# Another layout for loading and transposing queries and keys in a fused attention, soft-MoE and feed-forward kernel

## The chip, the cores and the metric

The kernel runs on one core of a Trainium2 chip. The metric is the device time of one execution in microseconds (us). A core has five engines with queues of their own: PE (TensorE, matrix products and transposes, results into PSUM), DVE (VectorE), ACT (ScalarE), POOL (GpSimd) and SP (SyncE, which here only issues transfers). Sixteen DMA engines move data between HBM and the on-chip memory, SBUF. Both on-chip memories have 128 partitions; an operand is so many partitions by so many elements. PEld is PE's loading of the stationary operand.

## The reference, cut to what matters

Three parts follow each other: an attention over q, k and v of shape (4 batches, 8 heads, 576 tokens, 64), a soft mixture of experts over its output, and a feed-forward layer. Only the first reads q and k:

```
q_d, k_d, v_d = means over 4 neighbouring tokens
out_d     = softmax(q_d k_d^T / 8) v_d              # 144 x 144 per head
scores    = q k^T / 8 where |i - j| < 4, else -1e9  # a band of 7
out_local = softmax(scores) v
out = repeat(out_d, 4 tokens) + out_local
x = out as (4 * 576 tokens, 8 heads * 64)
x = soft_moe(x; phi, w1, w2)          # 8 experts, 4 slots each
y = relu(x w_in)^2 w_out
```

The products need q and k with the 64 channels of a head on the partitions and tokens along the free dimension, while HBM holds a token's channels side by side. So q and k are transposed on the chip.

## The kernel before

The attention works on sixteen units; a unit is two heads of one batch. A loop takes a step for each unit, and a step works on several units at once: it transposes unit s, computes scores of unit s-1 and the values of units s-2 and s-3. The order of the work inside a step is written out by hand as a string of letters, `ORDER = "VDTAQL4gSpsEvdmqwenGtNlc"`; each engine gets its instructions in that order and runs them in order. The letters that matter here:

- `Q` (`load_qk`, lines 333 to 342): SP issues the loads of q and k of unit s+2, one each. A load brings 576 tokens of both heads to 96 partitions, three blocks of two neighbouring tokens per head on each, so that a contiguous run is two tokens, 512 bytes. There are two buffers for q and two for k, so the load waits until the transposes of unit s have read theirs.
- `L` and `4` (`load_v`, `load_v4`): SP issues the windows of v that the local attention reads (two loads in runs of 256 bytes) and the v block that is averaged over four tokens (runs of 2 KB) for unit s-1. `l` issues two or three weight loads for the experts and the feed-forward part, 512 KB each. SP's queue is served in order, so all of these stand in one line.
- `T` (`transposes`, lines 375 to 387): for q and k and each head, three transposes of 96 partitions into one PSUM bank, then two copies to SBUF, one for the even and one for the odd tokens, each 64 partitions by 288 elements, written with a step of two elements. ACT makes six of the eight copies, DVE the two of the second head's k. The PSUM buffers of the tag "t" are three banks, which the transposes share with the letters `p`, `q` and `t` (probabilities and outputs).
- `d` (line 389): POOL sums four neighbouring tokens of the transposed q and k. It stands behind `v` in POOL's queue (line 480, first sum of the v block, which waits for the load of `4`); `w` (line 486, DVE) is its second sum, and `D` (line 521, PE) multiplies with it.
- `S` (line 409): the local scores on PE; on DVE their maxima (417) and differences (418), on ACT their exponential `E` (423). `A` (line 534, DVE) adds the two attentions' values; it stands behind the copies of `T` on DVE. `g` and `G` (lines 602 to 630), every fourth step, gather the slot inputs of a finished batch. `c` converts pieces of the feed-forward weights on DVE, a number per step that a table gives.

Queries and keys are written into `qs[u % 2]`, both heads on 128 partitions, and `kzs[u % 2]`, where each head has columns of its own, with zeros on the other head's partitions. Columns 3 to 578 hold the 576 tokens in order. A table of units before the loop (`START`) does the first three units (T0, T1, T2), `DRAIN` the work after the last. Then follow the experts and the feed-forward part, which take the rest of the time.

Of the kernel before, what the change touches and what calls it, by code (L numbers as in the profile page):

```python
# [9 lines left out]
F32 = mybir.dt.float32  # L10
# [8 lines left out]
B, H, S, D = 4, 8, 576, 64  # L19
# [50 lines left out]
def attention_moe_ffn_kernel(  # L70
# [12 lines left out]
    nc = tc.nc  # L83
    cp = ctx.enter_context(tc.tile_pool(name="const", bufs=1))
    ring = ctx.enter_context(tc.tile_pool(name="ring", bufs=1))
# [5 lines left out]
    def bank(tag, shape, bufs, name, dt=F32):  # L91
        return ps.tile(shape, dt, tag=tag, bufs=bufs, name=name)

    def bt(shape, name):
        return bank("t", shape, 3, name)
# [4 lines left out]
    ident = cp.tile([128, 128], F32, name="ident")  # L100
# [5 lines left out]
    for g in range(4):  # L106
        r = slice(32 * g, 32 * g + 32)
# [186 lines left out]
    with tc.tile_pool(name="att", bufs=1, side="right") as ap:  # L294
        NV = 2
        vws, qs, kzs = [], [], []
        for i in range(NV):

            t = ap.tile([128, NB, D], F32, name=f"vw{i}")
# [3 lines left out]
        for i in range(2):  # L303
            t = aq.tile([128, SP + 6], F32, name=f"q{i}")
# [4 lines left out]
            t = aq.tile([128, 2, SP + 6], F32, name=f"kz{i}")  # L309
# [23 lines left out]
        def load_qk(u):  # L333
            b, hp = divmod(u, NP)
            h0 = 2 * hp
            st = U[u]
            for nm, src in (("q", q), ("k", k)):

                t = ring.tile([128, 1024], F32, tag=f"{nm}{u % 2}", name=f"{nm}{u}")[0:96, 0:768]
                t = t.rearrange("p (h a c) -> p h a c", h=2, a=3)  # L340
                nc.sync.dma_start(out=t, in_=src[b, h0:h0 + 2].rearrange("h (a p r) d -> p h a (r d)", a=3, r=2))
                st[nm] = t

        def load_v(u):
# [29 lines left out]

        def transposes(u):
            st = U[u]
            for j, nm in enumerate("qk"):
                for h in range(2):

                    t = bt([128, 3, 96], f"tr{u}_{j}{h}")  # L380
                    for i in range(3):
                        nc.tensor.transpose(t[:, i], st[nm][:, h, i], ident[0:96, 0:96])  # L382
                    hr = slice(64 * h, 64 * h + 64)
                    to = (kzs[u % 2][hr, h] if j else qs[u % 2][hr])[:, 3:3 + S].rearrange("p (i c r) -> p i c r", i=3, r=2)
                    for r in range(2):
                        copy = nc.vector.tensor_copy if j and h else nc.scalar.copy
                        copy(out=to[:, :, :, r], in_=t[64 * r:64 * r + 64])  # L387

        def downsample(u):
            eng = nc.vector if u in DDVE else nc.gpsimd  # L390
# [258 lines left out]
        def gate_rows(b):  # L649
# [6 lines left out]
            else:  # L656
# [8 lines left out]
                nc.vector.tensor_tensor(out=ctt_lo, in0=m, in1=ctt_hi, op=ALU.subtract)  # L665

        load_qk(0)
        for x in LOADS.split():
            if x[0] == "l":
                load_next(int(x[1:]))  # L670
            elif x == "phi":
                nc.sync.dma_start(out=phis, in_=phi.rearrange("(c p) s -> p c s", p=128))
            else:
                dict(Q=load_qk, L=load_v)[x[0]](int(x[1:])) if x[0] != "4" else load_v4(int(x[1:]))
# [3 lines left out]
        tm.enter_context(tc.manual_schedule())  # L678
        step = {
            "V": values, "T": transposes, "D": values_down, "A": value_adds, "Q": load_qk,  # L680
            "L": load_v, "S": scores_local, "p": probs_local, "E": exp_local, "s": scores_down, "d": downsample,
            "v": value_sums, "m": max_down, "q": probs_down, "e": exp_down, "n": norm_local, "N": norm_down,
# [52 lines left out]
        t = bt([1, 128], "mtp")  # L735
# [4 lines left out]
        t = bt([128, 2], "mbp")  # L740
# [23 lines left out]
        t = bt([128, 4, 32], "stp")  # L764
# [47 lines left out]
    for i in range(2):  # L812
        t = xp.tile([128, 2, 4, NS], F32, name=f"ht{i}")
# [221 lines left out]
    for i in range(2, len(steps) + LOOK):  # L1035
        up = lambda name, shape: pf.tile(shape, F32, tag="up", bufs=2, name=name)
        for x in SLOTS.get(i, ()):
            j = int(x[1:])
# [6 lines left out]
        if i < len(steps):  # L1045
            c, f = steps[i]
# [38 lines left out]
```

## Time and profile before

| | |
|---|---|
| Time, median of 3 runs | 465.41 us (463.23 to 468.02) |
| The profiled execution | 468.44 us, of which its span (first to last instruction) 466.7 us |
| PE busy | 423.5 us (91%) |
| DVE busy | 307.8 us (66%) |
| ACT busy | 262.0 us (56%) |
| POOL busy | 113.9 us (24%) |
| Mean granted clock of PE | 0.96 |
| DMA | 75.20 MB in 63,852 packets: 24,250 under 512 bytes, 42,938 under 2 KB |

The profile is of one execution on the chip. An instruction has a line of the kernel, an engine and the tiles that it writes and reads (`tr<-ident,k`: writes tr, reads ident and k). Idle time of an engine before an instruction is put down to what released it. Busy shares are averages over the whole span, in which the attention is less than half; so the views that follow are of stretches of it. The granted clock is the share of full speed that PE's throttle gave.

### The profile page before, as it was taken

The page shows a single profiled execution, that of the slowest core. Times are in us where ns is not written, and L with a number is a line of the kernel's source. Part 1 is how long each engine was busy: PE and PEld are TensorE (multiplying, and loading weights), DVE is VectorE, ACT ScalarE, POOL GpSimd, SP SyncE. Part 2 cuts the span into 40 slices and gives each one's busy share as a digit, 9 for nine tenths or more (in the row PEclk, how much of TensorE's full clock was granted, in tenths as well). Part 3 has the DMA queues.
Part 4 walks back from the last instruction along what each step waited for, and adds up shares of the span by engine and source line. Part 5 has one row for each costly group of instructions (what it writes and reads, how often), then busy time and mean ns, then how long its engine had stood idle before and what let it go on. Part 6 is the DMA issues. An engine that isn't in the chain of part 4 may idle for free.

```text
span 466.7 us, 10636 instructions
## 1 busy us (share of the span) xinstructions
PE 423.5 (91%) x4098; PEld 324.4 (70%) x4098; DVE 307.8 (66%) x655; ACT 262.0 (56%) x665; POOL 113.9 (24%) x173
## 2 busy tenths in 40 slices
PE   6489879886997988999869999999999999999996
PEld 5377666675675665454547787788888888888885
DVE  5488778796999993142398999946545555446542
ACT  5358765555676642124569897885445445444442
POOL 5158666655867840011000000000000000000000
PEclk9789979898999899899998999999999999999999
DMA  9999999999999978999996000003001001001001
GB/s 181 198 314 212 219 236 215 198 240 242 277 232 232 266 236 269 400 399 388 409 409 256 0 2 0 2 0 136 0 0 70 0 2 67 0 1 68 2 1 67
DMA packets 63852, 75.20 MB, mean 161 GB/s; under 512 B 24250, under 2 KB 42938, under 8 KB 63802
## 3 DMA queue, kind: packets, MB, share of 16 engines
q1 hardware_dynamic: 63658, 74.39, 58.4%
q8 instruction: 32, 0.52, 0.5%
q14 instruction: 18, 0.15, 0.1%
q10 hardware_dynamic: 144, 0.13, 0.1%
HBM read 69.79 MB, written 4.72 MB: 160 GB/s over the span
## 4 chain that ended last, share of the span: by engine, by line
PE 55%; DVE 20%; DMA 15%; issue 3%; ACT 3%; POOL 2%; SPq 1%; DVEq 0%; POOLq 0%; ACTq 0%
PE po L1014 37%; DMA v<-in_v_dram 13%; PE hp L822 4%; PE so L846 3%; PE up L954 3%; DVE win L217 2%; POOL v L480 2%; DVE win L218 2%; DVE vd L486 2%; DMA k<-in_k_dram 1%; DVE sm L450 1%; DVE glo L967 1%; DVE w L217 1%; DVE xt L534 1%; DVE win L215 1%
## 5 line engine op out<-in xcount | busy, mean ns | idle before, releaser
L1014 PE MATMUL po<-wparts,ghi 128*128 128x512 f32 x576 | 150.5, 395 | 4.3 <-DVE wparts L912 4.1
L1014 PEld LDWEIGHTS po<-wparts,ghi 128*128 128x128 f32 x576 | 107.2, 189 | 26.7 <-DVE wparts L912 6.6
L959 ACT ACTIVATE r<-up 128x384 f32<-128x384 f32 x96 | 47.0, 490 | 71.9 <-PE up L954 67.0
L1014 PE MATMUL po<-wparts,glo 128*128 128x512 f32 x288 | 82.2, 393 | 0.5 <-DVE glo L967 0.5
L963 DVE TENSOR_TENSOR r<-r 128x384 f32<-128x384 f32 x64 | 35.6, 557 | 58.6 <-ACT ghi L962 58.6
L967 DVE TENSOR_TENSOR glo<-r,ghi 128x384 fp32r<-128x384 f32 x94 | 52.3, 557 | 16.5 <-ACT ghi L966 10.3
L1014 PEld LDWEIGHTS po<-wparts,glo 128*128 128x128 f32 x288 | 54.3, 189 | 12.5 <-DVE glo L967 1.1
L962 ACT ACTIVATE ghi<-r 128x384 fp32r<-128x384 f32 x66 | 34.7, 526 | 2.1
L954 PE MATMUL up<-cst,ast 128*128 128x384 f32 x96 | 33.1, 346 | 0.4 <-DVE ast L945 0.4
L387 ACT COPY q<-tr 64x288 f32<-64x288 f32 x64 | 26.7, 418 | 10.9 <-PE tr L382 10.1
L480 POOL TENSOR_TENSOR v<-v 72x512 f32<-72x512 f32 x16 | 21.3, 1333 | 31.7 <-DMA v<-in_v_dram 31.7
L459 POOL TENSOR_TENSOR pl<-el,sm 64x350 f32<-64x350 f32 x30 | 26.0, 867 | 10.2 <-PE xrp L564 4.8
L387 DVE COPY kz<-tr 64x288 f32<-64x288 f32 x32 | 14.6, 457 | 14.9 <-PE tr L382 14.5
L382 PE MATMUL tr<-ident,k 96*128 96x96 f32 x96 | 16.4, 294 | 8.6 <-ACT q L387 8.3
L382 PE MATMUL tr<-ident,q 96*128 96x96 f32 x96 | 13.4, 285 | 9.7 <-DMA q<-in_q_dram 5.4
L508 PE MATMUL av<-pt,vw 64*64 64x58 f32 x640 | 22.0, 219 | 0.1
L508 PEld LDWEIGHTS av<-pt,vw 64*64 64x64 f32 x640 | 19.9, 135 | 2.9 <-issue 1.8
L954 PEld LDWEIGHTS up<-cst,ast 128*128 128x128 f32 x96 | 18.1, 189 | 4.6 <-DVE ast L945 0.7
L395 POOL TENSOR_TENSOR s<-kz 64x288 f32<-64x288 f32 x30 | 20.4, 678 | 2.3
L475 ACT COPY pt<-ptp 128x512 f32<-128x512 f32 (+1 forms) x32 | 12.1, 429 | 15.5 <-PE ptp L474 15.5
L382 PEld LDWEIGHTS tr<-ident,k 96*128 96x128 f32 x96 | 11.3, 165 | 12.0 <-ACT q L387 11.3
L467 POOL TENSOR_TENSOR pd<-pd,sm 128x432 f32<-128x432 f32 x16 | 16.4, 1028 | 10.9 <-DVE sm L451 9.9
(188 smaller groups left out, 714.2 us busy)
## 6 DMA issues: line engine op xcount, KB each, us to landing
w<-in_moe_w_dram SPq DMA_DIRECT2D x64, 512.0 KB, 8.1
win<-in_moe_w_in_dram SPq DMA_DIRECT2D x16, 512.0 KB, 9.0
wout<-in_moe_w_out_dram SPq DMA_DIRECT2D x16, 512.0 KB, 10.5
vw<-in_v_dram SPq DMA_DIRECT2D x30, 160.0 KB, 6.0
q<-in_q_dram SPq DMA_DIRECT2D x16, 288.0 KB, 10.3
k<-in_k_dram SPq DMA_DIRECT2D x16, 288.0 KB, 5.7
out_dram<-o SPq DMA_DIRECT2D x17, 256.0 KB, 2.2
v<-in_v_dram SPq DMA_DIRECT2D x16, 256.0 KB
```

Source lines behind the costliest of these rows:

```text
L382: nc.tensor.transpose(t[:, i], st[nm][:, h, i], ident[0:96, 0:96])
L387: copy(out=to[:, :, :, r], in_=t[64 * r:64 * r + 64])
L395: eng.tensor_tensor(out=s1[r], in0=t[:, :, 0], in1=t[:, :, 1], op=ALU.add)
L459: (nc.vector if u in NDVE else nc.gpsimd).tensor_tensor(out=pl[r, :, c0:c0 + W], in0=el[r], in1=sm[r, 0:NB].unsqueeze(2).to_broadcast([64, ...
L480: nc.gpsimd.tensor_tensor(out=v4[:, :, 0], in0=v4[:, :, 0], in1=v4[:, :, 1], op=ALU.add)
L508: nc.tensor.matmul(av[a][rr, 2 * HQ * i:2 * HQ * i + 2 * HQ].rearrange("p (f c) -> p f c", f=2), vw[rr, 2 * i + a], ptv[rr, i, :, a, 0:HQ] ...
L954: nc.tensor.matmul(t, ast[:, 128 * f:128 * f + 128], cst[:, c * n:c * n + n], start=True, stop=True)
L959: nc.scalar.activation(out=r, in_=t, func=AF.Relu)
L962: nc.scalar.activation(out=ghi, in_=r, func=AF.Square)
L963: nc.vector.tensor_tensor(out=g, in0=r, in1=r, op=ALU.mult)
L967: nc.vector.tensor_tensor(out=glo, in0=g, in1=ghi, op=ALU.subtract)
L1014: nc.tensor.matmul(po[c][i], a[:, 128 * i:128 * i + 128], w[f], start=(f == 0 and w is whi and a is ghi), stop=(f == NF - 1 and a is glo), ...
```

## The change

q and k of a unit are loaded to all 128 partitions: partition p of a head (64 partitions for each of the two heads) gets tokens 9p to 9p+8, one contiguous run of 2,304 bytes. A transpose then takes one token of the nine for both heads: 128 partitions by 64 channels become 64 partitions by 128 columns, of which 64 belong to each head. Four such transposes fill one PSUM bank, interleaved, so that four neighbouring tokens stand side by side; each writes every fourth word. Copies take 64 partitions by 256 elements for one head, in runs of four tokens with a step of nine. The ninth token has a tile for itself, for q and k together, written without gaps; DVE copies it in four pieces of 64 elements. A unit has eighteen transposes where it had twelve, five PSUM tiles where it had four, and twelve copies where it had eight.

```diff
             for nm, src in (("q", q), ("k", k)):
 
-                t = ring.tile([128, 1024], F32, tag=f"{nm}{u % 2}", name=f"{nm}{u}")[0:96, 0:768]
-                t = t.rearrange("p (h a c) -> p h a c", h=2, a=3)
-                nc.sync.dma_start(out=t, in_=src[b, h0:h0 + 2].rearrange("h (a p r) d -> p h a (r d)", a=3, r=2))
+                t = ring.tile([128, 1024], F32, tag=f"{nm}{u % 2}", name=f"{nm}{u}")[:, 0:9 * D]
+                nc.sync.dma_start(out=t, in_=src[b, h0:h0 + 2].rearrange("h (p t) d -> (h p) (t d)", t=9))
                 st[nm] = t
...
         def transposes(u):
             st = U[u]
+            to = []
+            for h in range(2):
+                r = slice(64 * h, 64 * h + 64)
+                to.append([x[:, 3:3 + S].rearrange("p (c t) -> p c t", t=9) for x in (qs[u % 2][r], kzs[u % 2][r, h])])
             for j, nm in enumerate("qk"):
-                for h in range(2):
-
-                    t = bt([128, 3, 96], f"tr{u}_{j}{h}")
-                    for i in range(3):
-                        nc.tensor.transpose(t[:, i], st[nm][:, h, i], ident[0:96, 0:96])
-                    hr = slice(64 * h, 64 * h + 64)
-                    to = (kzs[u % 2][hr, h] if j else qs[u % 2][hr])[:, 3:3 + S].rearrange("p (i c r) -> p i c r", i=3, r=2)
-                    for r in range(2):
+                for t0 in (0, 4):
+
+                    t = bt([64, 128, 4], f"tr{u}_{j}{t0}")
+                    for i in range(4):
+                        nc.tensor.transpose(t[:, :, i], st[nm][:, D * (t0 + i):D * (t0 + i) + D], ident)
+                    for h in range(2):
                         copy = nc.vector.tensor_copy if j and h else nc.scalar.copy
-                        copy(out=to[:, :, :, r], in_=t[64 * r:64 * r + 64])
+                        copy(out=to[h][j][:, :, t0:t0 + 4], in_=t[:, 64 * h:64 * h + 64])
+            t = bt([64, 2, 128], f"tr{u}")
+            for j, nm in enumerate("qk"):
+                nc.tensor.transpose(t[:, j], st[nm][:, 8 * D:9 * D], ident)
+            for h in range(2):
+                for j in range(2):
+                    nc.vector.tensor_copy(to[h][j][:, :, 8], t[:, j, 64 * h:64 * h + 64])
```

## Rows read from the trace of the kernel before

**Rows 1.** The page's chain that ended last: shares of the span by line.
```profile
PE po L1014 37%; DMA v<-in_v_dram 13%; PE hp L822 4%; PE so L846 3%; PE up L954 3%; DVE win L217 2%; POOL v L480 2%; DVE win L218 2%; DVE vd L486 2%; DMA k<-in_k_dram 1%; DVE sm L450 1%; DVE glo L967 1%; DVE w L217 1%; DVE xt L534 1%; DVE win L215 1%
```

**Rows 2.** Stretches: length; PE, PEld, DVE, ACT, POOL busy; clock, DMA share, GB/s.
```profile
38.20:46.30 8.10, 7.66 (x147) 6.14 (x145) 6.98 (x17) 6.43 (x20) 6.90 (x11) 1.00 1.04 227
54.60:123.10 68.50, 57.66 (x896) 43.20 (x894) 54.37 (x116) 40.47 (x131) 44.19 (x59) 0.88 1.13 226
...
131.60:140.30 8.70, 7.86 (x147) 6.17 (x145) 8.43 (x16) 6.42 (x20) 5.14 (x8) 1.00 1.09 237
```

**Rows 3.** Waits from 54.6 to 123.1: us in total, times, longest.
```profile
POOL v L480 <- DMA v<-in_v_dram: 21.0, 6, 4.6
```

**Rows 4.** Timeline, 63 to 88 us: start, length, line, work, [idle before, releaser].
```profile
68.63 1.22 SPq L158 DMA_DIRECT2D w<-in_moe_w_dram  x2
...
71.65 4.22 SPq L358 DMA_DIRECT2D vw<-in_v_dram  x2
...
73.29 1.06 PE L620 MATMUL sip<-xk,ee 128*32 128x512 f32 x8
...
74.28 1.12 PE L626 MATMUL sip<-xr,etr 64*128 64x512 f32 x2
...
75.96 2.89 SPq L372 DMA_DIRECT2D v<-in_v_dram  x2
...
85.44 1.26 POOL L480 TENSOR_TENSOR v<-v 72x512 f32<-72x512 f32 x1 [3.54 <-DMA v<-in_v_dram]
```

**Rows 5.** Timeline of SP's issues from 9 to 20 us.
```profile
13.50 1.50 SPq L341 DMA_DIRECT2D k<-in_k_dram  x1
```

**Rows 6.** Stretches, with the columns of rows 2; the last is GB/s.
```profile
15.30:17.50 2.20, 0.00 (x0) 0.00 (x0) 0.00 (x0) 0.00 (x0) 0.00 (x0) 0.91 1.22 229
71.00:73.00 2.00, 2.00 (x20) 1.47 (x19) 1.86 (x5) 0.81 (x3) 0.00 (x0) 0.82 1.09 256
125.50:127.50 2.00, 2.00 (x46) 1.50 (x35) 1.94 (x6) 1.53 (x4) 0.98 (x1) 1.00 1.04 383
```

**Rows 7.** Timeline of SP's issues from 117 to 126 us.
```profile
121.33 2.34 SPq L158 DMA_DIRECT2D w<-in_moe_w_dram  x3
```

**Rows 8.** Timeline of the step from 38.2 us, PE, ACT and DVE.
```profile
38.23 0.71 PE L382 MATMUL tr<-ident,q 96*128 96x96 f32 x6
...
38.74 1.72 ACT L387 COPY q<-tr 64x288 f32<-64x288 f32 x4
38.78 0.41 PE L382 MATMUL tr<-ident,k 96*128 96x96 f32 x3
...
39.93 0.31 PE L403 MATMUL s<-maskb,identb 128*128 128x350 bf16 x1
...
40.13 0.93 DVE L387 COPY kz<-tr 64x288 f32<-64x288 f32 x2 [0.72 <-PE tr L382]
...
43.07 0.50 ACT L423 ACTIVATE el<-el 128x350 f32<-128x350 f32 x1 [0.65 <-DVE el L418]
```

**Rows 9.** Timeline of PE, 160 to 187 us: a transpose, then bf16 matmuls.
```profile
177.24 0.27 PE L564 MATMUL xrp<-ident,xt 128*64 128x128 f32 x1
177.35 0.82 PE L328 MATMUL warm<-identb 128*128 128x256 bf16 x6
```

**Rows 10.** Timeline, 462.3 us on: two engines read halves of one PSUM bank.
```profile
462.79 0.37 ACT L1024 COPY o<-po 128x256 f32<-128x256 f32 x1
...
463.19 0.42 DVE L1026 COPY o<-po 128x256 f32<-128x256 f32 x1 [1.07 <-ACT o L1024]
```

**Rows 11.** DVE's groups by form to 185 us: count, busy us, mean ns, idle before.
```profile
L387 DVE COPY kz<-tr 64x288 f32<-64x288 f32 x32 | 14.6, 457 | 14.9 <-PE tr L382 14.5
...
L575 DVE COPY lst<-lgt 128x16 f32<-128x16 f32 x4 | 0.6, 162 | 0.0
```

**Rows 12.** Timeline of PE to 31 us: the third and the fourth unit.
```profile
17.85 1.19 PE L382 MATMUL tr<-ident,q 96*128 96x96 f32 x6 [5.40 <-DMA q<-in_q_dram]
...
30.14 0.71 PE L382 MATMUL tr<-ident,q 96*128 96x96 f32 x6
```

## The prediction, made before the changed kernel ran

> **What bounds the kernel now.** I read the chain of waits first, to see which stage can pay. The largest items are TensorE's (PE) in the experts and the feed-forward part, and nothing there reads a query or a key: the change is worth what it does to the sixteen head pairs ("units") before them. Of those the chain's largest item is a load of v, 13% of the span [rows 1]. So the question is whether the DMA rings or an engine pace a step, and the table by stretch answers it. From 38 to 46 us a step takes 8.1 us and PE is busy for 7.66 of them at full clock: PE paces. The six steps from 54.6 to 123.1 us take 68.5 us, 11.4 each, with the rings full (share 1.13 at 226 GB/s), and PE is throttled part of the time (mean grant 0.88). A later step, 8.7 us, is VectorE's (DVE): 8.43 busy [rows 2]. The waits say how the rings pace the middle: GpSimd waits 21.0 us in six waits for the v block [rows 3], whose sums DVE and PE need next. The timeline says why: in the SyncE queue (SP) the v block stands behind the same step's q, k and windows of v. The two window issues hold SP 4.22 us, the v block goes out at 75.96 and is first used at 85.44, nearly a step later [rows 4]. Fewer or larger packets ahead of it bring it earlier.
>
> **What the middle would take without the rings.** Four plain steps at 8.1 us, and two with the gather of slot inputs, which adds 1.06 + 1.12 us of matmuls and two transposes of 0.11, so 10.5 [rows 2, 4, 9]: 4 × 8.1 + 2 × 10.5 = 53.4 of 68.5 us. The rings, and the throttled clock beside the idle time, cost 15.1 us.
>
> **DMA.** A unit's q and k are 2 × 294,912 bytes. Today they go in 512-byte rows; after, in 2,304-byte rows. From 15.3 to 17.5 us q and k are what is in flight (SP's last four issues are q, k, q, k, the last at 13.50), at 229 GB/s [rows 5, 6]: 1.29 us a load. The nearest rows for the new size are 2 KB rows of expert weights, issued just before: 256 GB/s from 71 to 73 us, 383 from 125.5 to 127.5 [rows 4, 6, 7]: 1.15 or 0.77 us. A unit saves 0.27 to 1.04 us; I take the middle, 0.66, since both rows lie in the same phase of the kernel. A gain of zero stays in the range: nothing of before shows a 2,304-byte row. The issues on SP stay two a unit. Before step 12, 14 units are loaded: 9.2 us of ring time.
>
> **PE.** Twelve transposes of 96 columns become eighteen of 128. Six of the former start within 0.55 us (38.23 to 38.78), 0.09 each [rows 8]; one of 128 columns is followed after 0.11 us [rows 9]. So 1.1 us becomes 2.0. Today the last three also wait for a PSUM buffer, and the local scores start 1.70 us after the first transpose (39.93). After, the fifth tile needs the buffer of the second, which ACT empties at 0.5 (where the q copies start today) + 4 × 0.39 = 2.1 us; with its two transposes the scores start at 2.5. PE: +0.8 a step.
>
> **Copies.** ACT keeps six, of 256 elements in place of 288: 0.37 to 0.42 us [rows 8, 10], no longer than today. DVE keeps two (0.42 for 256, [rows 10]) and gains four of 64 elements. Today's copies of 16 and of 288 elements take 0.16 and 0.46 [rows 11], so 0.21 each: +0.8 us of DVE a step. There is also a new order. ACT and DVE read two halves of one PSUM bank; where the kernel does that today, DVE starts when ACT has ended (462.79 + 0.37, then 463.19) [rows 10]. So the second k copy on DVE starts at about 3.0 us of the step and the four small ones end at 4.4, where DVE is through at 2.8 today (40.13 + 0.93 against 38.23). Behind them on DVE wait the sums with v and the reductions of the scores, and ACT's exponential, which already waits 0.65 us for DVE [rows 8], comes 1.5 us later. ACT's chain then closes a loop of about 9.0 us. A step that neither rings nor conversions bound: 8.1 + 0.95 = 9.05.
>
> **The sum**, on the profiled execution (468.44 us, span 466.7; the median of the three runs is 465.41, so 3.0 lower).
> 1. Start: T2, the third unit, waits for q until 17.85 [rows 12]; five loads before it save 5 × 0.33 = 1.65. Its transposes are slower there, six in 1.19, so twelve in 2.4; eighteen of 128 columns take up to 18/12 × 128/96 = 2 times that, and about 3.9 without the fill that each run has once: +1.5, and DVE's copies +0.5. Net +0.3: the fourth unit starts at 30.4 for 30.1.
> 2. Steps 3 to 5: 3 × 9.05 = 27.2.
> 3. Steps 6 to 11: 4 × 9.05 + 2 × 11.45 = 59.1. That puts step 12 at 116.7. By the rings alone it would be 123.1 − 9.2 = 113.9. Two bounds this close take turns in a queue served in order; I add 2.5 us, a sixth of today's 15.1, by my judgement. 119.2 for 123.1: −3.9.
> 4. Steps 12 to 15 are DVE's, nothing covers its copies: 4 × 0.85 = +3.4.
> 5. Behind the last unit nothing changes: weight loads are issued a fixed number per step, and the experts start when the units end.
>
> Together (the +0.3 is inside the −3.9) −3.9 + 3.4 = −0.5: **465 us** in terms of the median, no change. What the rings give back, PE and DVE spend.
>
> **Rivals.** *Slower: the scattered PSUM write.* Sixteen of the eighteen transposes write every fourth word. No matmul of before does. For a cost: nothing in the trace excludes one. Against: a transpose of 128 columns takes 0.11 us, and so does a bf16 matmul of 256 columns (six in 0.82, one alone 0.27) [rows 9], so a transpose writes at half the rate that the port has shown, and a write of twice the price would still fit. If each took double: 16 × 0.11 = 1.76 us more a step; steps 3 to 5 +5.3, the middle 59.1 + 10.6 against 68.5, +1.2, steps 12 to 15 PE's at 10.7, +8; three start units, at point 1's 3.9 / 18 = 0.22 a transpose, 3 × 16 × 0.22 = 10.5 less the 5.4 that PE waits there anyway, +5: 19.5 in all, 485 us. It decides from about 0.14 us a transpose, where PE alone paces every step. The Trainium skill, PSUM — Partial Sum Buffer, Specifications (TRN2), says just this: lines of 8 bytes, and any non-contiguous pattern slows matmuls significantly; no run here shows it yet.
>
> *Faster: the rings give the upper end and copies don't queue.* At 1.04 us a unit the rings let step 12 come at 108, well under PE's path; the 2.5 us go, the start gains 1 more, and if DVE need not wait for ACT a step is 8.9 for 9.05, 13 × 0.15 = 2: 5.5 less than the forecast's sum, 459.4 us. For it: the 383 GB/s row. Against: the ordered pair at the end of the kernel.
>
> *The load gains nothing.* If the rings pay by bytes in this phase (256 GB/s for 2 KB rows beside 229 says nearly so), the middle keeps its 68.5 us, whose waits hide the new work; the start (+2.0), steps 3 to 5 (+2.8) and 12 to 15 (+3.4) pay: +8.2, 473.6 us.
>
> **How the numbers follow.** Forecast 0.48, with its own range 460 to 471 (relief of 0.27 to 1.04 us a unit; hit of 0 to 5 us); scattered write 0.17; upper end 0.20; no gain 0.15. One per cent, 4.65 us, is about what a measurement here can tell from no change. Faster by more: 0.15 of the upper end, 0.12 of the forecast's low side: 0.27. Slower by more: 0.17, 0.12 of no gain, 0.03: 0.32. Within: 0.41. The range 457 to 477 leaves out most of the scattered write and a larger gain than I can derive.
>
> **What would show it.** Packets of q and k at 2,304 bytes and a rate over 229 GB/s where they are alone; GpSimd's 21.0 us of waits for v cut to a third; step 12's transposes near 119.2 us for 123.1; transposes 0.11 us apart, scores 2.5 us after the first; DVE's second k copy behind ACT's; steps 12 to 15 at 9.4 us; the experts starting within 2 us of today's time. Wrong would be: transposes 0.2 us apart (slower), the v waits unchanged (no gain), or the DVE-bound steps no longer than before, which would mean that the conversions had slack I don't see.

## The result, and the profile after

The changed kernel takes 469.84 us (median of 20 runs, 467.99 to 472.51) where the kernel before took 467.7 (20 runs on the same chip, 463.23 to 471.66). The ratio is 1.0093, with an interval of 1.0071 to 1.0115: slower by 0.9%, or 4.3 us. Ratios here count only the faster executions of each kernel, which is why 1.0093 is more than the 2.1 us between these two medians, and the profiles of e5, e9 and e11 below are of executions that are not counted, so that their late step times may be too high. The forecast was 465.0, no change against the 465.41 us of the first three runs; the time lies in its range, but the forecast's 0.5 us less came out as 4.3 us more, and the rival with a price nearest to it (no gain from the load, 473.6) is not what happened. The profiled execution after took 470.22 us with a span of 468.4, before 468.44 and 466.7: this pair of profiles is only 1.7 us apart, and the experiments must speak for the rest.

The chain that ended last, from the page after, against [rows 1]:
```profile
PE po L1021 39%; PE hp L829 4%; PE tr L385 4%; PE so L853 3%; PE up L961 3%; PE av L515 2%; DVE xt L541 2%; ACT q L388 2%; DVE kz L388 2%; DVE win L217 2%; DVE win L215 1%; DVE win L218 1%; DVE q L394 1%; PE av L528 1%; DVE el L425 1%
```
The load of v, 13% before, is gone from the list. In its place stand short pieces of TensorE (PE), VectorE (DVE) and ScalarE (ACT), among them the new copies (L388, L394) and the transposes (L385). Packets under 2 KB fell from 42,938 to 24,506.

Stretches after, with the columns of [rows 2]: two plain steps, steps 6 to 11, steps 12 to 14, and a stretch of the last units' work.
```profile
38.30:47.70 9.40, 8.92 (x153) 6.87 (x151) 8.41 (x23) 6.56 (x22) 6.90 (x10) 1.00 0.89 248
47.70:57.10 9.40, 8.92 (x153) 6.87 (x151) 7.47 (x21) 6.34 (x20) 6.81 (x10) 1.00 0.85 234
57.10:119.10 62.00, 57.69 (x933) 42.50 (x931) 52.24 (x135) 39.81 (x131) 43.17 (x57) 1.00 0.89 248
119.10:129.10 10.00, 8.94 (x154) 6.86 (x152) 9.34 (x22) 6.25 (x20) 6.08 (x9) 1.00 0.87 235
129.10:139.50 10.40, 8.99 (x154) 6.91 (x153) 9.75 (x24) 6.27 (x20) 6.81 (x10) 1.00 0.87 243
139.50:150.30 10.80, 8.86 (x153) 6.83 (x151) 10.41 (x23) 6.25 (x20) 6.81 (x10) 1.00 0.96 258
172.00:179.00 7.00, 6.88 (x79) 5.55 (x78) 3.30 (x8) 1.84 (x5) 1.18 (x1) 0.54 0.53 188
```
A plain step is 9.4 us long for 8.1, with the transfers at 0.85 to 0.89 for 1.04. Steps 6 to 11 took 62.0 us for 68.5, at a clock of 1.00 for 0.88. Steps 12 to 14 took 10.0, 10.4 and 10.8 us (before 8.5, 8.7 and 10.7). Within the middle, step 9 (87.2 to 97.8) is a plain one too, but took 10.7 us: weight conversions on DVE, from 87.41 to 91.20, stand ahead of k's copies there.

Waits after in steps 6 to 11, against [rows 3]:
```profile
POOL s L402 <- DVE kz L394: 8.0, 6, 2.3
ACT el L430 <- DVE el L425: 7.9, 6, 1.6
...
POOL v L487 <- DMA v<-in_v_dram: 0.5, 1, 0.5
```
GpSimd (POOL) waits 0.5 us for v where it waited 21.0. Two waits for DVE have come in or grown: POOL's sums of q and k for the ninth token's copies, ACT's exponential for the differences.

The plain step from 47.7 us after, PE, ACT and DVE, against [rows 8]:
```profile
47.73 1.06 PE L385 MATMUL tr<-ident,q 128*64 128x128 f32 x8
...
50.07 0.69 ACT L388 COPY kz<-tr 64x256 f32<-64x256 f32 x2
...
50.34 0.31 PE L410 MATMUL s<-maskb,identb 128*128 128x350 bf16 x1
...
50.51 0.75 DVE L388 COPY kz<-tr 64x256 f32<-64x256 f32 x2 [1.50 <-ACT kz L388]
...
51.29 0.27 DVE L394 COPY q<-tr 64x64 f32<-64x64 f32 x1
...
51.43 0.26 DVE L394 COPY kz<-tr 64x64 f32<-64x64 f32 x1
51.70 0.27 DVE L394 COPY q<-tr 64x64 f32<-64x64 f32 x1
51.85 0.25 DVE L394 COPY kz<-tr 64x64 f32<-64x64 f32 x1
...
54.11 0.50 ACT L430 ACTIVATE el<-el 128x350 f32<-128x350 f32 x1 [1.27 <-DVE el L425]
```
Eight transposes fill 1.06 us, the last with its own 0.27, so they start 0.11 us apart, as on contiguous columns [rows 9]. The local scores start 2.61 us after the first transpose. DVE's copies of k wait 1.50 us, released by ACT's copies on the same bank; the four small ones follow, 0.25 to 0.27 us each but overlapping, so that all four pass in 0.81 us (51.29 to 52.10). The exponential starts 6.38 us into the step, where it was 4.84 (43.07 less 38.23).

### The profile page after: what moved, and what is told of

Read it like the earlier page. It is cut to its first block, busy times and chain, and to the rows that moved or that the text cites. A ratio compares the mean times of both kernels' runs of the same rounds, so it can differ in the third digit from the quotient of the medians.

```text
span 468.4 us, 10907 instructions
## 1 busy us (share of the span) xinstructions
PE 434.4 (93%) x4194; PEld 330.2 (70%) x4194; DVE 312.0 (67%) x719; ACT 259.3 (55%) x665; POOL 114.3 (24%) x173
## 4 chain that ended last, share of the span: by engine, by line
PE 64%; DVE 24%; ACT 6%; issue 4%; DMA 2%; POOL 1%; DVEq 0%; ACTq 0%; POOLq 0%
PE po L1021 39%; PE hp L829 4%; PE tr L385 4%; PE so L853 3%; PE up L961 3%; PE av L515 2%; DVE xt L541 2%; ACT q L388 2%; DVE kz L388 2%; DVE win L217 2%; DVE win L215 1%; DVE win L218 1%; DVE q L394 1%; PE av L528 1%; DVE el L425 1%
## 5 line engine op out<-in xcount | busy, mean ns | idle before, releaser
L1021 PEld LDWEIGHTS po<-wparts,ghi 128*128 128x128 f32 x576 | 107.1, 189 | 26.8 <-DVE wparts L919 6.5
L974 DVE TENSOR_TENSOR glo<-r,ghi 128x384 fp32r<-128x384 f32 x94 | 52.3, 557 | 16.5 <-ACT ghi L973 10.4
L388 ACT COPY q<-tr 64x256 f32<-64x256 f32 x64 | 25.7, 402 | 7.8 <-PE tr L385 6.2
L466 POOL TENSOR_TENSOR pl<-el,sm 64x350 f32<-64x350 f32 x30 | 23.3, 775 | 19.6 <-DVE sm L458 10.8
L388 DVE COPY kz<-tr 64x256 f32<-64x256 f32 x32 | 12.1, 414 | 18.1 <-ACT kz L388 17.9
L487 POOL TENSOR_TENSOR v<-v 72x512 f32<-72x512 f32 x16 | 23.2, 1451 | 1.1 <-DMA v<-in_v_dram 1.0
L515 PE MATMUL av<-pt,vw 64*64 64x58 f32 x640 | 23.0, 225 | 0.2
L385 PE MATMUL tr<-ident,q 128*64 128x128 f32 x128 | 17.8, 284 | 5.8 <-POOL maskf L197 3.7
L515 PEld LDWEIGHTS av<-pt,vw 64*64 64x64 f32 x640 | 20.9, 140 | 2.6 <-DVE xt L541 0.6
L385 PE MATMUL tr<-ident,k 128*64 128x128 f32 x128 | 20.3, 285 | 1.6 <-ACT q L388 1.1
L961 PEld LDWEIGHTS up<-cst,ast 128*128 128x128 f32 x96 | 18.1, 189 | 4.6 <-DVE ast L952 0.7
L430 ACT ACTIVATE el<-el 128x350 f32<-128x350 f32 x16 | 7.9, 497 | 23.8 <-DVE el L425 23.8
L385 PEld LDWEIGHTS tr<-ident,q 128*64 128x64 f32 x128 | 13.3, 115 | 8.8 <-POOL maskf L197 3.6
## 6 DMA issues: line engine op xcount, KB each, us to landing
wout<-in_moe_w_out_dram SPq DMA_DIRECT2D x16, 512.0 KB, 10.4
```

Source lines behind the costliest of these rows:

```text
L385: nc.tensor.transpose(t[:, :, i], st[nm][:, D * (t0 + i):D * (t0 + i) + D], ident)
L388: copy(out=to[h][j][:, :, t0:t0 + 4], in_=t[:, 64 * h:64 * h + 64])
L466: (nc.vector if u in NDVE else nc.gpsimd).tensor_tensor(out=pl[r, :, c0:c0 + W], in0=el[r], in1=sm[r, 0:NB].unsqueeze(2).to_broadcast([64, ...
L487: nc.gpsimd.tensor_tensor(out=v4[:, :, 0], in0=v4[:, :, 0], in1=v4[:, :, 1], op=ALU.add)
L515: nc.tensor.matmul(av[a][rr, 2 * HQ * i:2 * HQ * i + 2 * HQ].rearrange("p (f c) -> p f c", f=2), vw[rr, 2 * i + a], ptv[rr, i, :, a, 0:HQ] ...
L961: nc.tensor.matmul(t, ast[:, 128 * f:128 * f + 128], cst[:, c * n:c * n + n], start=True, stop=True)
```

## Experiments

Each ratio is to the kernel before, run on the same chip beside it. Steps are counted by the first transpose of each.

| | to unit 4 | steps 3–5 | 6–11 | 12–14 | rest of span | span | ratio |
|---|---|---|---|---|---|---|---|
| before | 30.1 | 24.5 | 68.5 | 27.9 | 315.7 | 466.7 | 1 |
| forecast | 30.4 | 27.2 | 61.6 | 30.5 | 316.5 | 466.2 | |
| after | 29.0 | 28.1 | 62.0 | 31.2 | 318.1 | 468.4 | 1.0093 |
| e4, ninth on ACT | 27.0 | 26.9 | 58.3 | 27.1 | 314.7 | 454.0 | 0.9805 |
| e9, loads alone | 28.0 | 24.3 | 62.8 | 26.6 | 317.7 | 459.4 | 0.9727 |
| e12, eight copies | 26.8 | 24.8 | 56.9 | 26.2 | 317.8 | 452.5 | 0.978 |

**e1. The kernel before, once more**, unchanged, one run.

> The kernel before, unchanged, profiled once more. Theory (the middle steps' loss to the rings varies from run to run, and the profile on record was an execution that lost more than the median): step 12's transposes start earlier than 123.1 us, 119 to 121, and the span is 2 to 4 us shorter than 466.7. Rival (the loss is the same in each execution, and the measured 0.9% comes from elsewhere): step 12 again within 1 us of 123.1.

468.1 us, span 466.3; step 12 at 120.2 (123.1), the experts at 187.01 (187.05). When the middle goes 3 us better, that is lost again before the experts start: step times of a single profile are good to some 3 us only. Behind step 15 this execution of the unchanged kernel took 317.7 us, 2.0 more than the first profile, and PE's granted clock, 1.00 there from 172 to 179 us, was 0.50 here:
```profile
172.00:179.00 7.00, 7.00 (x82) 5.40 (x78) 1.84 (x5) 1.15 (x3) 0.00 (x0) 0.50 0.43 153
```
So neither a slow clock nor some 2 us more in that part is a mark of the change.

**e2. Longer runs for the kernel before.** Six tokens (1,536 bytes) a partition on its 96 partitions.
```diff
-  t = t.rearrange("p (h a c) -> p h a c", h=2, a=3)      # source "h (a p r) d -> p h a (r d)", a=3, r=2
+  t = t.rearrange("p (h c) -> p h c", h=2)               # source "h (p r) d -> p h (r d)", r=6
...
-  to = (...)[:, 3:3 + S].rearrange("p (i c r) -> p i c r", i=3, r=2)
+  to = (...)[:, 3:3 + S].rearrange("p (c i r) -> p i c r", i=3, r=2)
```


> The kernel before with one part alone: q and k loaded in longer rows (six neighbouring tokens of a head on each of 96 partitions, rows of 1,536 bytes for 512). Twelve transposes of 96 columns, four tiles and eight copies of 288 as before; only the step of the copies' writes grows from two to six elements. Theory (rows set the ring time, and the engines' loop without the change's extra work is 8.1 us): GpSimd's waits for v in the middle fall from 21 us to under 8, plain steps take 8.1 to 8.6 us, step 12 starts at 107 to 113, ratio to before 0.972 to 0.985. Rival (the rings pay by bytes, or by v's 256-byte windows alone): step 12 at 120 or later, ratio 0.995 to 1.003.

Ratio 1.0135 (1.0084 to 1.0185): slower, where the theory expected a gain, because the edit did a second thing. Copies by form:
```profile
L387 ACT COPY q<-tr 64x288 f32<-64x288 f32 x64 | 43.4, 679 | 7.6 <-PE tr L382 6.8
...
L387 DVE COPY kz<-tr 64x288 f32<-64x288 f32 x32 | 22.1, 690 | 20.7 <-PE tr L382 20.4
```
The copies now write every sixth element, 24 bytes apart, and 288 elements cost 0.68 (ACT) and 0.69 us (DVE) where a step of 8 bytes cost 0.42 and 0.46 ([rows 11]): 0.9 and 0.8 ns an element more. A plain step became 9.65 us. On the loads this run says nothing; e5 repeats it without the side effect. On the queue it does: with these longer steps, steps 6 to 11 took 62.5 us at a clock of 1.00, with 4.9 us of waits for v.
```profile
59.10:121.60 62.50, 51.97 (x896) 38.15 (x894) 51.18 (x111) 50.59 (x131) 43.33 (x56) 1.00 1.01 225
POOL v L480 <- DMA v<-in_v_dram: 4.9, 2, 3.0
```
At 8.1 us a step the same loads leave 27.0 us of such waits (e5). A slower plain step by itself lets the queue keep up, so the middle of the changed kernel, 62.0 us, is no proof of better loads.

**e3. No bank shared by two engines.** ACT copies k's first bank alone, DVE the second.
```diff
-  copy = nc.vector.tensor_copy if j and h else nc.scalar.copy
+  copy = nc.vector.tensor_copy if j and t0 else nc.scalar.copy
```


> The changed kernel, but both heads of the first k tile are copied by ACT and both heads of the second by DVE, so that no PSUM bank is read by two engines; the number of copies per engine stays (ACT six, DVE two and four). Theory (part of the step is the order between the two engines on one bank): DVE's k copies no longer wait for ACT, plain steps 9.0 to 9.2 us for 9.4, ratio to before 1.002 to 1.006. Rival (the DVE work or PE's transposes set the step, not the order): 9.4 us stays, ratio 1.008 to 1.011.

Ratio 0.9965 (0.9924 to 1.0006), plain steps 9.0 us. DVE's idle time ahead of these copies fell from 18.1 us in the whole run, 17.9 of them for ACT, to 13.0, 12.8 of them for PE:
```profile
L388 DVE COPY kz<-tr 64x256 f32<-64x256 f32 x32 | 12.1, 414 | 18.1 <-ACT kz L388 17.9
```
```profile
L388 DVE COPY kz<-tr 64x256 f32<-64x256 f32 x32 | 13.3, 416 | 13.0 <-PE tr L385 12.8
```
Against the changed kernel's 1.0093 that is 1.3% or 5.9 us. DVE's wait for ACT on one bank cost more than I expected. Whether the chip or the kernel's own semaphores order the two engines, no run here shows.

**e4. The ninth token's four copies on ACT.**
```diff
-  nc.vector.tensor_copy(to[h][j][:, :, 8], t[:, j, 64 * h:64 * h + 64])
+  nc.scalar.copy(out=to[h][j][:, :, 8], in_=t[:, j, 64 * h:64 * h + 64])
```


> The changed kernel, with the four copies of the ninth token on ACT instead of DVE. Theory (the step's loop runs through DVE's copies, and steps 12 to 15 are DVE's): plain steps 8.9 to 9.1 us, steps 12 to 14 under 9.8, ratio to before 0.992 to 0.998. Rival (ACT is as tight as DVE, or PE's eighteen transposes pace the step): plain steps stay at 9.3 to 9.5 and ratio 1.006 to 1.012.

Ratio 0.9805 (0.9727 to 0.9882), 456.91 us, better than expected: one line turns the loss into a gain of 2%, and against the changed kernel it is worth 2.9%, 13.4 us. The chain of one plain step shows why. First the changed kernel's, start, length and work of the pieces that released each other:
```profile
47.80 1.45 PE tr L385 x12
...
49.65 0.40 ACT q L388
...
50.07 0.41 ACT kz L388
...
50.51 0.75 DVE kz L388 x2
...
51.29 0.27 DVE q L394
...
51.70 0.27 DVE q L394
...
52.13 0.83 DVE xt L541 x2
52.96 0.44 DVE mx L424
...
53.49 0.53 DVE el L425
...
54.51 0.38 ACT pdt L503
...
54.94 0.30 PE xrp L571
55.23 1.31 PE av L515 x40
```
and the same of e4:
```profile
45.00 1.44 PE tr L385 x12
...
46.85 0.41 ACT q L388
...
47.30 0.41 PE tr L391 x2
...
47.85 0.74 PE s L416 x40
...
49.29 0.88 PE sd L438 x12
...
52.01 1.31 PE av L515 x40
```
In the changed kernel the step runs through all three engines: ACT's copies, DVE's copies of k, the four small ones (51.29 to 52.10, 0.81 us), the sum with v, the maxima, the differences, then ACT's exponential and the copy behind it (`pdt`, L503), after which PE's `xrp` and the product with v start, and then the next step. In e4 that loop is off the chain, and but for one wait on ACT's copies of q PE paces a step of 9.0 us. The forecast followed this loop as far as the exponential, and took it for 9.0 us. The kernel before had little room behind it, as its own step shows ([rows 8], the same step):
```profile
43.47 0.38 ACT L496 COPY pdt<-pdp 72x288 f32<-72x288 f32 x1
...
44.18 0.27 PE L564 MATMUL xrp<-ident,xt 128*64 128x128 f32 x1
```
ACT's first copy of `pdt` ended at 43.85, and PE came to `xrp` at 44.18 without a wait. Of 1.54 us by which the exponential comes later, 0.3 fit in there, and the step is 1.3 us longer.

Steps 12 to 14 fell too, from 31.2 to 27.1 us. In e3, whose plain step is also 9.0 us, they still take 30.6, with DVE busy for 29.15 of them (24.33 of 27.1 in e4): where DVE is the limit, the four copies that stay on it are paid in full. That is 3.5 of the 7.2 us between the two spans, in one profile each.

**e5. Longer runs again, copies as before.** The transposes of a bank write interleaved, so that the copies keep their step of two elements.
```diff
   nc.sync.dma_start(out=t, in_=...rearrange("h (p r) d -> p h (r d)", r=6))     # as in e2
-  nc.tensor.transpose(t[:, i], st[nm][:, h, i], ident[0:96, 0:96])
+  nc.tensor.transpose(t[:, :, i], st[nm][:, h, 128 * i:128 * i + 128], ident[0:96, 0:96])
...
+  copy(out=to[:, :, r], in_=t[64 * r:64 * r + 64].rearrange("p c i -> p (c i)"))   # to: "p (m r) -> p m r"
```


> The kernel before with loads in runs of six neighbouring tokens (1,536 bytes) instead of two, and the three transposes of a bank written interleaved (every third word), so that the eight copies have the shape and the write step of two elements that they had before. Theory 'longer runs relieve the DMA queue, and only the copies ate it': a plain step stays at 8.1 us, a copy costs 0.42 (ACT) and 0.46 us (DVE) as before, the excess of steps 6 to 11 falls to about the 5.6 us that the changed kernel shows over six plain steps (62.0 - 6 x 9.4), the transposes of step 12 start at 107 to 113 us (before 123.1), ratio 0.965 to 0.985. Rival 'the queue is bound by its bytes and not by its runs': steps cannot shrink below what they take now, the waits for v stay near 21 us in the stretch of steps 6 to 11, step 12 starts at 118 us or later, ratio 0.99 to 1.00. Rival 'transposes that write scattered words cost PE time': transposes more than 0.11 us apart, a plain step of 8.5 us or more.

Ratio 1.0169 (1.0097 to 1.024). The copies are back at 0.418 and 0.458 us and a plain step at 8.1, so transposes that write every third word cost nothing. But the waits for v in the middle are 27.0 us and step 12 comes at 128.5: runs three times as long relieve nothing on 96 partitions. Why it is even slower than the kernel before stays open.

**e8. Shorter runs on 128 partitions.** The changed kernel's tiles filled in three runs of 768 bytes a partition.
```diff
-  nc.sync.dma_start(out=t, in_=src[b, h0:h0 + 2].rearrange("h (p t) d -> (h p) (t d)", t=9))
+  runs = bass.AP(tensor=hs.tensor, offset=hs.offset, ap=[[3 * D, 128], [384 * D, 3], [1, 3 * D]])
+  nc.sync.dma_start(out=t.rearrange("p (x y) -> p x y", x=3), in_=runs)
```


> The changed kernel with q and k loaded in three runs of 768 bytes per partition instead of one of 2,304 bytes: the same bytes into the same tiles, three times as many packets (the tokens that land there are not the right ones; everything else is as in the changed kernel). Theory 'what the change gained in steps 6 to 11 (62.0 us for 68.5) it gained through longer runs': part of the waits for v comes back (5 to 12 us in that stretch), step 12 starts at 121 to 125 us, ratio to the kernel before 1.013 to 1.025. Rival 'the gain is from somewhere else, such as fewer loads that wait for buffers': step 12 at 118.5 to 120, ratio 1.007 to 1.012.

Ratio 1.0125 (1.0064 to 1.0185), step 12 at 120.8, and the step lengths of the changed kernel (9.4 plain). The ratio lies between the two expectations, and so does step 12; the waits for v that the first one needs did not come back (1.6 us in steps 6 to 11, 0.5 after, 21.0 before). The rate with nothing but q and k in flight separates runs from partitions. Stretches in which the third unit waits for its loads, GB/s last: 1,536 bytes on 96 partitions (e2), 768 bytes on 128 (e8), 2,304 bytes on 128 (after); [rows 6] has 229 for 512 bytes on 96.
```profile
15.00:17.00 2.00, 0.00 (x0) 0.00 (x0) 0.00 (x0) 0.00 (x0) 0.81 (x2) 1.00 1.07 265
```
```profile
14.00:16.50 2.50, 0.13 (x2) 0.16 (x3) 1.28 (x3) 0.49 (x1) 2.19 (x5) 1.00 1.04 313
```
```profile
14.00:15.70 1.70, 0.00 (x0) 0.00 (x0) 1.41 (x4) 0.49 (x1) 1.47 (x4) 1.00 1.05 387
```
Half the run length on a third more partitions is faster (313 for 265; e5, whose loads are those of e2, had 235 from 15 to 18 us). The run length counts too, 387 for 313. For the Trainium skill, SBUF — State Buffer, Door 1: The DMA port swizzle, a transfer's rate hangs on how many of sixteen ports its partitions reach, eight for partitions 0 to 63 and the other eight for 64 to 127. Worked out from that, 96 partitions send two thirds of their bytes through half the ports, an estimate of three quarters of the full rate. These rows agree in direction; 96 partitions with runs of 2,304 bytes were not tried.

**e9. The loads alone.** The kernel before, every transpose and copy as it was, with the changed kernel's loads.
```diff
-  nc.sync.dma_start(out=t, in_=src[b, h0:h0 + 2].rearrange("h (a p r) d -> p h a (r d)", a=3, r=2))
+  nc.sync.dma_start(out=t, in_=src[b, h0:h0 + 2].rearrange("h (p t) d -> (h p) (t d)", t=9))
...
-  nc.tensor.transpose(t[:, i], st[nm][:, h, i], ident[0:96, 0:96])
+  c0 = 88 * (3 * h + i)
+  nc.tensor.transpose(t[:, i], st[nm][0:96, c0:c0 + 128], ident[0:96, 0:96])
```


> The kernel before, all its transposes and copies as they were, with nothing but the changed kernel's loads (128 partitions, one run of 2,304 bytes each); the transposes take overlapping pieces of those rows, so the tokens are not the right ones. Theory 'the queue is relieved by the spread over 128 partitions and not by the length of the runs' (all transfers took 49.9 and 50.0% of the span with 2,304- and 768-byte runs on 128 partitions, 58.4 and 57.7% with 512- and 1,536-byte runs on 96): plain steps stay at 8.1 us, the waits for v in steps 6 to 11 fall from 21 us to under 8, the transposes of step 12 start at 106 to 113 us (before 123.1), ratio 0.955 to 0.98, transfers 50 to 54% of the span. Rival 'the changed kernel's steps 6 to 11 are smooth because its plain steps of 9.4 us leave the queue more time': at 8.1 us a step the waits for v stay near 20 us, step 12 starts at 118 us or later, ratio 0.985 to 1.005.

Ratio 0.9727 (0.9671 to 0.9783): the loads are worth 2.7%, 12.7 us. The six times spread widely, from 452.51 to 465.35 us, and the medians of all executions, 459.64 and 466.97, would give 0.984. Plain steps stay at 8.1 us:
```profile
44.20:52.30 8.10, 7.64 (x147) 6.13 (x145) 6.91 (x15) 6.53 (x20) 5.45 (x7) 1.00 1.06 264
52.30:115.10 62.80, 54.59 (x897) 40.78 (x895) 51.97 (x112) 40.82 (x131) 43.97 (x58) 0.92 1.00 250
```
A plain step of the same 8.1 us now moves 264 GB/s, for 227 in [rows 2]. Step 12 comes at 115.1; the waits for v in the middle are still 15.5 us, so the queue remains a limit at this pace: the ratio is as the theory said, the waits are not, and step 12 misses its 106 to 113. The rest of the change, transposes and copies, therefore costs 1.0093 - 0.9727 = 3.7%, 17 us by the ratios (2.0% by the medians of all executions), of which e4 recovers 13.4.

**e6. e3 and e4 together**, both diffs above.

> The changed kernel with both edits tried before at once: the ninth token's four copies on ACT, and k's first bank copied by ACT alone and its second by DVE alone. Theory 'two separate costs on DVE (its four small copies; its wait for ACT's copy of the same bank)': each edit took 0.4 us off a plain step of 9.4, both take about 0.7: plain step 8.6 to 8.8, step 12 at 109 to 111 us, ratio 0.968 to 0.977. Rival 'both edits remove the same wait, DVE's late arrival at the maxima': plain step stays 9.0 as with either alone, ratio 0.977 to 0.985.

Ratio 0.9863 (0.9804 to 0.9922), plain steps of 9.0 us: the rival, with the ratio just above its range. Both edits remove DVE from the same chain, and once PE paces the step the second one has nothing left to win.

**e7. Throw-away products in the last units' work** (`f5` and the like in the table of units behind the loop).
```diff
-  "... V14 t13 D14 A14 c1 v15 p15 w15 q15 V15 ..."
+  "... V14 t13 f5 D14 f5 A14 c1 v15 p15 f4 w15 q15 V15 ..."
```


> The changed kernel with 14 throw-away products on PE placed in the last units' work behind the loop (5, 5 and 4, ahead of waits of PE). Theory 'part of the loss behind step 15 is the clock: PE runs at 0.50 to 0.66 from 172 to 179 us in the changed kernel and at 1.00 before': the granted clock of that stretch rises above 0.8, the experts' first products start 1.0 to 1.7 us earlier relative to the transposes of step 15 (37.0 us after them instead of 37.7, before 36.0), and their 0.77 us come back too; ratio to the kernel before 1.003 to 1.007. Rival 'the clock follows from waits that would be there anyway': the clock rises but the experts start no earlier, ratio 1.008 to 1.012; or the fillers stand in the way, ratio above 1.012.

```profile
172.00:179.00 7.00, 5.77 (x102) 4.50 (x98) 3.65 (x11) 2.06 (x7) 0.42 (x1) 1.00 0.63 237
179.00:187.00 8.00, 7.10 (x49) 3.96 (x52) 2.49 (x11) 1.21 (x7) 0.57 (x2) 0.84 0.93 322
```
The granted clock of 172 to 179 us is 1.00 (0.54 in the changed kernel), and the experts' products start 35.8 us after step 15's transposes, not 37.7. But those products then take 6.49 us (6.10 after, 5.35 before), and the ratio, 1.0083 (1.0044 to 1.0121), can't be told from 1.0093. The slow clock is shown, and e1 shows it without the change; that it costs the whole kernel anything is not shown.

**e10. Two tokens per transpose** (128 x 128, ten transposes, three tiles, eight copies of 256, the ninth on ACT).
```diff
-  for i in range(4):   # for each t0 in (0, 4)
-      nc.tensor.transpose(t[:, :, i], st[nm][:, D * (t0 + i):D * (t0 + i) + D], ident)
+  for i in range(4):
+      nc.tensor.transpose(t[:, :, i], st[nm][:, 2 * D * i:2 * D * i + 2 * D], ident)
...
+  copy(out=to[h][j][:, :, r:8:2], in_=t[64 * r:64 * r + 64, 64 * h:64 * h + 64])
```


> The changed kernel's loads, but transposes of two tokens of both heads (128 x 128) instead of one: four for q, four for k, two for the ninth tokens, ten instead of eighteen; three PSUM tiles instead of five; eight copies of 64 x 256 (pairs written with a step of two elements inside runs of nine) and the ninth token's four on ACT. Theory 'PE is the bound of a plain step once DVE is relieved' (the run with the ninth token on ACT: PE busy 61.4 of 63 us, steps of 9.0 us, transposes 2.8 us of it): the transposes' stretch falls to about 1.9 us, a plain step to 8.2 to 8.6 us, step 12 at 105 to 110 us, ratio 0.955 to 0.975. Rival 'copies whose inner write step is 8 bytes inside a step of 36 cost as the 24-byte step did, about 0.6 us for 256': ACT's queue sets the step, 9.2 us or more, ratio 0.985 to 1.01.

Ratio 0.9971 (0.9929 to 1.0013), plain steps 9.2 us. The transposes fell to 1.3 us, more than expected, but the step did not follow. Step and ratio are the rival's; its reason is not, for a copy costs 0.42 us. In the middle PE waits 6.0 us, in six waits, for ACT's copies of the ninth token before its transposes of the probabilities, and DVE 11.0 us for ACT on k's bank. Less PE work moved the pace to ACT.

**e11. e10 with DVE's copies of k ahead of ACT's.**
```diff
-  for h in range(2):
+  for h in ((1, 0) if j else (0, 1)):
```

> As the run with pairs, and for k's bank DVE's two copies stand ahead of ACT's two. Theory 'DVE's copies of k wait for ACT's on the same bank, and PE's scores for DVE's': DVE's wait of 1 to 2 us per unit disappears, the scores start 0.2 to 0.5 us earlier, ratio 0.003 to 0.02 below that of the run with pairs. Rival 'PE or the DMA queue sets the step by then': ratio within 0.004 of the run with pairs.

Ratio 0.9874 (0.9826 to 0.9922), 1.0% below e10, in the theory's range. DVE's wait for ACT is gone and the plain steps before the first gather fell to 8.3 us, but the scores start no earlier (1.15 us after the first transpose, e10 1.14). The twelve times run from 458.85 to 472.47 us, and their median, 466.84, is above e10's 464.93: that e11 is the faster of the two is not shown. In its profile ACT waits at the gather steps for DVE, which converts weights, and part is lost again.

**e12. The loads, and eight copies.** A tile for each tensor and head as before; the ninth token goes into the fifth column of the even ones. These lines stand in place of the changed kernel's two tiles a tensor and its tile for the ninth tokens.
```diff
+  t = bt([128, 64, 5], f"tr{u}_{j}{h}")
+  for i in range(5):
+      w = 2 * D if i < 4 else D
+      nc.tensor.transpose(t[0:w, :, i], st[nm][hr, 2 * D * i:2 * D * i + w], ident[hr, hr])
+  for r in range(2):
+      copy = nc.vector.tensor_copy if j and h else nc.scalar.copy
+      copy(out=to[h][j][:, :, r:9:2], in_=t[64 * r:64 * r + 64, :, 0:5 - r])
```


> The changed kernel's loads, but one PSUM tile per tensor and head, as the kernel before had: four transposes of two tokens and one of the ninth (64 partitions each, twenty in all, written interleaved) fill 64 x 5 columns, so that the eight copies of before remain (320 elements for the even, 256 for the odd tokens of a run of nine, six on ACT, two on DVE) and no copy is for the ninth token alone. Theory 'the change is worth its loads and costs its extra copies': with the copies back to eight, a plain step is 8.1 to 8.4 us, step 12 at 106 to 116 us, ratio 0.965 to 0.982, as the run of the kernel before with these loads (0.9727). Rival 'transposes of nine tokens cost PE, however they are copied' (the run with ten transposes and the ninth copied by ACT had steps of 9.2 us): a step of 8.7 us or more, ratio 0.985 to 1.00. Rival 'copies of 320 elements in runs of nine cost as the 24-byte step did, 0.7 us': ratio above 1.00.

Ratio 0.978 (0.9724 to 0.9837), 455.25 us: with e4 the best of these, and it beats both kernels.
```profile
43.30:51.60 8.30, 7.66 (x156) 6.15 (x154) 6.85 (x18) 6.58 (x20) 6.85 (x10) 1.00 1.01 276
51.60:108.50 56.90, 51.97 (x944) 39.01 (x942) 48.13 (x111) 41.52 (x131) 42.51 (x56) 0.97 1.09 270
```
As the theory had it: with twenty transposes of nine tokens a plain step takes 8.3 us, so it was not the transposes that cost, but the additional copies. Its 276 GB/s are the most of the plain steps shown here, and step 12 comes at 108.5, where the prediction's upper end for the queue had put it (108).

## Why the prediction was wrong, point by point

- **What bounds the kernel: right.** The queue paced the middle, and better loads relieve it: e9 gains 2.7%, and its step 12 at 115.1 is near the 113.9 "by the rings alone".
- **DMA: in the range, wrong reason.** Assumed: longer runs, 1.29 us a load down to 1.15 or 0.77, and a gain of 0.66 us a unit. Measured: 294,912 bytes at 387 GB/s, 0.76 us, so 1.06 us a unit, the upper end. e5 and e8 show that the partitions have the larger part in it: on 96 of them a run three times as long brought 235 to 265 GB/s and no gain.
- **PE: right.** Transposes 0.11 us apart, scores 2.61 us after the first (forecast 2.5).
- **Copies: right.** DVE goes behind ACT on one bank; the small copies end 4.4 us into the step, where the forecast had them; the exponential comes 1.5 us later, as it said. One small copy takes 0.25 to 0.27 us, not 0.21 (it writes at a step of 36 bytes, the rows used for it contiguous or at 8), but they overlap, and the four pass in 0.81 us for the forecast's 0.84.
- **The step, "a loop of about 9.0 us": the term that failed.** The forecast put 0.95 us on a step, 9.05; it is 1.3, 9.4 (three plain steps: 28.1 for 27.2). It stopped at the exponential and took about 0.6 us of the 1.5 as absorbed, without a row for it. Behind the exponential the chain goes on through ACT's copy of `pdt`, PE's `xrp` and the product with v into the next step, and there the kernel before had only 0.3 us to spare (e4). Moving the four copies off DVE brings the step to 9.0 and the kernel to 456.91 us, so this loop is what turned the result. POOL's wait for the ninth token's copies, 8.0 us in the middle, was not foreseen either, but does not stand on the chain of the step shown.
- **Steps 6 to 11: right total (62.0 for 61.6), wrong parts.** No hits by the queue (0.5 us of waits for v, forecast 2.5 us of hits) but longer steps, among them the 10.7 us of step 9: at 9.4 us the queue keeps up, and by e2 it nearly does so with loads on 96 partitions. That the total came out is luck. The gain of the loads was there and could not be used.
- **Steps 12 to 15 at +0.85 each: too low.** 12 to 14 took 3.3 us more, not 2.6: there DVE's conversions come first and the whole loop behind them. With the four copies on ACT (e4) nothing is left of it.
- **"Behind the last unit nothing changes": not decided.** Behind step 15's first transpose the span is 2.4 us longer, with 0.85 foreseen, and PE's granted clock was 0.54 for 7 us there, close to the lower of its two levels (1.2 GHz), where the first profile of before has 1.00. But e1 shows the unchanged kernel with 2.0 us more in that part too, and a clock of 0.50; and e7 undid the slow clock without a gain that can be measured. What the change does there is not shown.
- **The rivals.** The scattered write to PSUM is refuted: 0.11 us a transpose for every fourth word here, no cost for every third word in e5. The rule of the Trainium skill quoted for it (PSUM — Partial Sum Buffer, Specifications (TRN2)) does not hold for these transposes; the measurement decides. "The load gains nothing" is refuted by e9. "Upper end and no queueing of copies" had the load right and the copies wrong; e12 is that case, 455 us for 459.4.

The sign hung on a difference: the loads' gain of 12.7 us against some 17 for the rest, each uncertain by a few us, and the forecast took the two for equal.

## What to carry to other kernels

A change of layout is two changes: how the load spreads over partitions, and how many pieces must then be put in place. Measure them apart, for the better version can keep the one without the other. Where a step is a loop through several in-order engines, follow its chain until it is back at the first engine before pricing it; a few short copies in that chain cost their whole length every time round, and the same copies on the engine beside it cost little. Work that is taken off the bound moves the bound: after e4 the split of k's banks brought nothing more.

## What the runs showed of the hardware that I had not expected

- A copy of fp32 from PSUM costs by its write step in SBUF: 288 elements 0.418 us (ACT) at 8 bytes, 0.679 at 24; 256 elements in runs of four with gaps 0.402. The Trainium skill, SBUF — State Buffer, Door 1: The DMA port swizzle, speaks of lines of 16 bytes, of which two or more accesses in a row should use the same. The three prices agree with it: two elements to a line, one, up to four.
- Transposes of fp32 that write every third or fourth word of a PSUM bank run at the pace of contiguous ones, 0.11 us.
- q and k alone in flight moved 229 GB/s (512 bytes on 96 partitions), 235 and 265 (1,536 on 96), 313 (768 on 128) and 387 (2,304 on 128).
